# Two heads' score products in the two row halves of TensorE, with readers that take two PSUM banks at once

## The chip, the cores and the metric

The kernel runs on one core of one Trainium2 chip. The core has five engines with instruction queues of their own: TensorE (PE in the profile, with its weight loads as PEld), VectorE (DVE), ScalarE (ACT), GpSimd (POOL) and SyncE (SP), which here issues nearly all DMAs. The metric is device time in microseconds (us) from one execution of the whole program; several executions are timed and their median is taken.

## What is computed

A transformer layer in fp32 on one sequence of 2048 tokens with 512 channels: layer norm, attention with 32 heads of 16 channels in a sliding window of 256 tokens, an output projection with a residual, a second layer norm, and a mixture of 8 experts of hidden size 1376, two for each token.

```python
def _A_ref(x, wqkv, wo):            # H = 32, Dh = 16, W = 256
    qkv = (x @ wqkv).reshape(B, S, 3, H, Dh).transpose(2, 0, 3, 1, 4)
    q, k, v = qkv[0], qkv[1], qkv[2]
    scores = jnp.einsum("bhqd,bhkd->bhqk", q, k) * (Dh ** -0.5)
    mask = (idx[:, None] - idx[None, :] >= 0) & (idx[:, None] - idx[None, :] < W)
    p = _softmax(jnp.where(mask[None, None], scores, -1e9), axis=-1)
    o = jnp.einsum("bhqk,bhkd->bhqd", p, v)
    return o.transpose(0, 2, 1, 3).reshape(B, S, D) @ wo

h = x + _A_ref(_layernorm(x), A_wqkv, A_wo)
out = h + _B_ref(_layernorm(h), B_wg, B_w1, B_w2)
```

`_B_ref` takes the two experts with the largest gates for each token, applies gelu(x w1) w2 for each, and adds them up with normalised gates.

## The kernel before, in words

Matrices are held as a high and a low part in fp32r, so that a dense product is three products (high·high, high·low, low·high). The sequence is cut into four chunks of 512 tokens, and attention into 32 units: chunk c of 4 with head group g of 8, four heads to a group. A last stage runs the experts one after another.

A unit goes through these steps:

- `qk(u)` (line 535): twelve matmuls of 512 columns make Q and K of the group; ACT and POOL split them into high and low, three DMAs write them to DRAM (lines 547 to 549), and four read them back in another layout into one of four slots (lines 555 and 560). In a slot, heads 0 and 2 lie on partitions 0 to 47 (16 channels, as three products), heads 1 and 3 on partitions 64 to 111. Q has a plane for each of the four heads, and is zero on the partitions of the other head of its pair; K has one plane for a pair of heads.
- `maxes(u)`: for each of four blocks of 128 queries and each head, a matmul over 126 partitions makes 128 × 384 scores (fewer in chunk 0) in one PSUM bank (line 588). DVE copies the part above the diagonal from the far block with a predicate (line 594), so that 256 columns hold just the window, and takes their maximum (line 597). `fin` (lines 604 to 606) splits the negated maxima into two parts and transposes them; a DMA writes them to DRAM (line 609), and another reads them back into partitions 126 and 127 of Q (line 612), where K holds ones. So the second score product already has the maximum subtracted.
- `attend(u)`: scores again, transposed, over all 128 partitions (line 636), in four tiles A to D of key blocks (three tiles in chunk 0). Each of `scores()`'s groups fills one bank; ACT takes the exponential into the tile `PT` (line 640), POOL zeroes what lies outside the window (line 660), and PE multiplies with V (line 676). This last product uses 17 columns for each of four heads, placed in four column strips of the array, and adds up in the bank `oT`.
- `norm_and_v(c)` (V at line 482) and `project(c)` (lines 748 and 851, with the routing of the experts) run once for each chunk, among the units.

The order of work is not written out: every step is a task with an engine, an estimated duration, a priority and the buffers it needs, and `Plan.order()` runs a list schedule over them and emits the instructions of each engine in the order it finds. Engines then run their queues in order and wait on semaphores. Buffers are counted in pools: seven single PSUM banks (`one`), of which groups of maxima may hold three (`mx`) and groups of scores three (`ab`); the other tasks take from the same seven. `oT` is the eighth bank. On all engines a task is issued only when its buffers are free, and the PSUM bank of a group of scores or maxima is free again when ACT or DVE has read it for the last time.

## Time and profile before

| | us |
|---|---|
| median of 3 runs | 1243.21 |
| lowest and highest | 1240.88 and 1250.29 |
| the profiled execution's own time | 1246.75 |
| its span, first to last instruction | 1244.7 |

| engine | busy, share of the span | instructions |
|---|---|---|
| PE | 1118.5 us, 90% | 6801 |
| PEld | 892.2 us, 72% | 6801 |
| DVE | 678.2 us, 54% | 1833 |
| ACT | 540.8 us, 43% | 1153 |
| POOL | 455.1 us, 37% | 668 |

Attention runs from the first matmuls to some 640 us (the last P·V ends there), the experts from about 644 us to the end. PE's "busy" counts a matmul from its start to its modelled end; matmuls overlap in the array, so a busy PE is not an array at its peak. "Idle before" of a group is the time its engine stood still ahead of it, with what ended that time. The granted clock is the share of TensorE's full clock that the throttle allowed; over the span it was 0.948.

### The profile page before, as it was taken

The page shows a single profiled execution, that of the slowest core. Times are in us where ns is not written, and L with a number is a line of the kernel's source. Part 1 is how long each engine was busy: PE and PEld are TensorE (multiplying, and loading weights), DVE is VectorE, ACT ScalarE, POOL GpSimd, SP SyncE. Part 2 cuts the span into 40 slices and gives each one's busy share as a digit, 9 for nine tenths or more (in the row PEclk, how much of TensorE's full clock was granted, in tenths as well). Part 3 has the DMA queues.
Part 4 walks back from the last instruction along what each step waited for, and adds up shares of the span by engine and source line. Part 5 has one row for each costly group of instructions (what it writes and reads, how often), then busy time and mean ns, then how long its engine had stood idle before and what let it go on. Part 6 is the DMA issues. An engine that isn't in the chain of part 4 may idle for free.

```text
span 1244.7 us, 19621 instructions
## 1 busy us (share of the span) xinstructions
PE 1118.5 (90%) x6801; PEld 892.2 (72%) x6801; DVE 678.2 (54%) x1833; ACT 540.8 (43%) x1153; POOL 455.1 (37%) x668
## 2 busy tenths in 40 slices
PE   1797989979898999998788999999999999999994
PEld 0574666657666676766357889889798897989893
DVE  4288567977787786776546144434243342434341
ACT  1335555434554445544555245425253351626240
POOL 4734544744556464653844411220302112020101
PEclk9998998999899898996887899999999999999997
DMA  3489799884799758777332634442534334353422
GB/s 114 112 239 274 207 243 275 252 197 89 190 260 263 179 120 213 197 214 183 108 118 75 144 104 123 113 82 89 120 115 122 87 107 87 105 130 112 105 66 29
DMA packets 111617, 185.51 MB, mean 149 GB/s; under 512 B 25092, under 2 KB 44612, under 8 KB 111508
## 3 DMA queue, kind: packets, MB, share of 16 engines
q1 hardware_dynamic: 102852, 166.42, 47.7%
q0 software_dynamic: 8656, 17.73, 7.7%
q8 instruction: 56, 0.92, 0.3%
q14 instruction: 53, 0.43, 0.1%
HBM read 124.51 MB, written 59.60 MB: 148 GB/s over the span
## 4 chain that ended last, share of the span: by engine, by line
PE 67%; DMA 17%; DVE 6%; SPq 3%; POOL 2%; issue 2%; ACT 1%; POOLq 0%; DVEq 0%; ACTq 0%
PE one L1139 21%; PE one L1118 21%; PE one L588 5%; PE one L535 5%; PE oT L676 4%; PE one L636 4%; DMA mr<-qkd 3%; PE one L748 2%; PE one L482 2%; DMA md<-mt 2%; DMA mr<-md 2%; DMA od<-zone 1%; PE one L851 1%; SPq L387 1%; DVE mx L597 1%
## 5 line engine op out<-in xcount | busy, mean ns | idle before, releaser
L640 ACT ACTIVATE zone<-one 128x384 f32<-128x384 f32 (+1 forms) x480 | 207.8, 494 | 155.2 <-PE one L636 131.7
L1118 PE MATMUL one<-mr 128*128 128x256 f32 (+7 forms) x1980 | 269.2, 298 | 0.0
L1118 PEld LDWEIGHTS one<-mr 128*128 128x128 f32 (+1 forms) x1980 | 266.7, 188 | 1.1
L1139 PE MATMUL one<-zone,mr 128*128 128x512 f32 (+3 forms) x1080 | 260.4, 397 | 0.0
L660 POOL TENSOR_SCALAR_AFFINE_SELECT zone<-zone 128x256 f32<-128x256 f32 (+1 forms) x368 | 169.5, 483 | 201.4 <-ACT zone L640 198.8
L1139 PEld LDWEIGHTS one<-zone,mr 128*128 128x128 f32 (+3 forms) x1080 | 193.3, 181 | 53.0
L363 DVE TENSOR_TENSOR mr<-one,mr 128x256 fp32r<-128x256 f32 (+9 forms) x205 | 100.5, 494 | 180.1 <-ACT mr L361 171.2
L597 DVE TENSOR_REDUCE mx<-one 128x1 f32<-128x256 f32 (+2 forms) x472 | 192.3, 426 | 0.8
L588 PE MATMUL one<-mr 126*128 126x384 f32 (+2 forms) x512 | 166.1, 376 | 19.9 <-DMA mr<-qkd 10.7
L636 PE MATMUL one<-mr 128*128 128x384 f32 (+1 forms) x592 | 152.9, 336 | 21.1 <-DMA mr<-md 11.2
L594 DVE COPY_PREDICATED one<-above,one 128x128 f32<-128x128 uint32 x448 | 120.8, 289 | 77.3 <-PE one L588 68.7
L588 PEld LDWEIGHTS one<-mr 126*128 126x128 f32 x512 | 95.7, 201 | 78.1 <-issue 25.9
L636 PEld LDWEIGHTS one<-mr 128*128 128x128 f32 x592 | 109.6, 204 | 48.6 <-DVE mx L597 17.0
L361 ACT CAST mr<-one 128x256 fp32r<-128x256 f32 (+9 forms) x205 | 87.6, 431 | 128.8 <-PE one L1090 113.6
L1085 POOL DMA_INDIRECT mf<-xnd,tb x36 | 35.1, 975 | 287.6 <-PE one L1090 271.4
L535 PE MATMUL one<-mr 128*128 128x512 f32 x384 | 108.8, 413 | 23.2 <-ACT mr L361 23.0
L361 ACT CAST mr<-mf 128x512 fp32r<-128x512 f32 (+4 forms) x120 | 93.2, 787 | 82.2 <-DMA mf<-in_B_w_dram 26.1
L1123 ACT ACTIVATE one<-one 128x256 f32<-128x256 f32 (+7 forms) x165 | 65.2, 395 | 142.7 <-PE one L1118 132.6
L1145 DVE TENSOR_SCALAR mf<-one,tb 128x512 f32<-128x512 f32 (+3 forms) x36 | 27.0, 750 | 173.2 <-PE one L1139 173.2
L1147 POOL DMA_INDIRECT out_dram<-mf,tb x36 | 61.5, 1708 | 162.2 <-DVE mf L1145 142.6
L676 PE MATMUL oT<-zone 128*17 128x384 f32 (+2 forms) x1408 | 110.9, 407 | 8.1 <-POOL zone L660 6.9
L365 POOL TENSOR_TENSOR mr<-mf,mr 128x512 fp32r<-128x512 f32 (+2 forms) x74 | 94.1, 1284 | 55.4 <-ACT mr L361 50.6
(141 smaller groups left out, 965.6 us busy)
## 6 DMA issues: line engine op xcount, KB each, us to landing
mf<-in_B_w_dram SPq DMA_DIRECT2D x32, 688.0 KB
mf<-in_B_w_dram SPq DMA_DIRECT2D x40, 512.0 KB
qkd<-mr SPq DMA_DIRECT2D x32, 512.0 KB
mr<-qkd SPq DMA_DIRECT2D x80, 192.0 KB
mr<-qkd SPq DMA_DIRECT2D x48, 288.0 KB
mr<-wgd SPq DMA_DIRECT2D x24, 512.0 KB
mf<-in_A_x_dram SPq DMA_DIRECT2D x32, 256.0 KB
qkd<-mr SPq DMA_DIRECT2D x64, 128.0 KB
```

The costliest lines, as they stand in the source:

```text
L361: a = add("ACT", 51 + n * 0.86, lambda: nc.scalar.copy(dst_h(), src()), deps, prio, bufs)
L363: b = add("DVE", 65 + n * 1.05, lambda: nc.vector.tensor_sub(dst_l(), src(), f32(dst_h())), [a], prio, bufs)
L535: nc.tensor.matmul(single[bk.h], wt()[:, int(i == 1), k * 128:(k + 1) * 128], xt[:, k], start=(i == 0 and k == 0), stop=(i == 2 and k == 3))
L588: nc.tensor.matmul(view()[:, j], Q[slot.h][0:126, h + j, b * 128:(b + 1) * 128], K[slot.h][0:126, (h + j) // 2, (b + k0) * 128:(b + 3) * 1 ...
L594: nc.vector.copy_predicated(t[:, :, n - 128:n], above.unsqueeze(1).to_broadcast([128, m, 128]), src)
L597: nc.vector.tensor_reduce(mx_t[slot.h][:, h:h + m, b], view()[:, :, max(0, n - 256):n], axis=AX.X, op=OP.max)
L636: nc.tensor.matmul(single[bk.h][:, off:off + w], K[slot.h][:, h // 2, r * 128:(r + 1) * 128], Q[slot.h][:, h:h + hs, b * 128:(b + m) * 128 ...
L640: return add("ACT", 51 + n * 0.833, lambda: nc.scalar.activation(dst(), single[bk.h][:, 0:n].rearrange(order, q=128, **({"h": 2} if "h" in ...
L660: nc.gpsimd.affine_select(v, v, pattern=[[0, v.shape[1]], [-1 if far else 1, 128]], compare_op=OP.is_gt if far else OP.is_ge, fill=0.0, ba ...
L676: nc.tensor.matmul(oT[32 * j:32 * j + 17, b * 128:(b + n) * 128], V[blk % NV][:, 4 * g + j, :], PT[pt.h][j // 2][:, off:off + n, j % 2], s ...
L1118: nc.tensor.matmul(bank(), a[:, k, f * 128:f * 128 + w], b[:, k, :n], start=(i == 0), stop=(i == 11))
L1139: nc.tensor.matmul(single[bk.h][:n], h[a][:w], spot["w2"][b][f][:w], start=(f == 0 and q == 0), stop=(f == NF - 1 and q == 2))
```

## The change

Q and K of a slot now hold both heads of a pair in one plane: head 2i on partitions 0 to 47, head 2i + 1 on partitions 64 to 111, without zeros between. A score product uses just the 48 partitions of its head (50 in `attend`, with the two rows of the maximum, which now lie behind each half at partitions 48 and 112). The two matmuls of a pair stand one behind the other in PE's queue, in row halves 0 and 64 of the array, and write to two neighbouring banks. Six of the seven banks become three tiles of two banks; a `Buf` of size 2 takes an even and the next odd place of the pool, and a `Buf` of size 1 prefers a place whose neighbour is taken. DVE's predicated copy and its maximum and ACT's exponential each take both banks in one instruction. `mx` and `ab` go from three to two. `PT` has its head dimension ahead of its block dimension, and POOL's selection and the P·V product are addressed to match. The read of the maxima is two DMAs of two rows each, and the write puts them down transposed. The zeroing of Q is gone.

```diff
@@ class Plan
-        def places(p, e):
-            return [f for f in self.free[p] if f[1] + self.HOP[f[2]][e] <= now]
+        def places(bufs, e):
+            out, used = [], set()
+            for b in bufs:
+                can = [f for f in self.free[b.pool] if f[1] + self.HOP[f[2]][e] <= now and (b.pool, f[0]) not in used]
+                at = {f[0]: f for f in can}
+                if b.size == 2:
+                    f = next(((f, at[f[0] + 1]) for f in can if f[0] % 2 == 0 and f[0] + 1 in at), None)
+                else:
+                    alone = [f for f in can if f[0] ^ 1 not in at]
+                    f = (alone or can)[:1]
...
@@ layer
-        Q.append(take(mr, 4, 512))
+        Q.append(take(mr, 2, 512))
         K.append(take(mr, 2, 768))
+        at[id(mr)] += 1024
-    PT = [[take(zone, 3, 2, 128) for _ in range(2)] for _ in range(NPT)]
+    PT = [[take(zone, 2, 3, 128) for _ in range(2)] for _ in range(NPT)]
-    single = [psum.tile([128, 512], F32, name=f"one{i}", bufs=1) for i in range(7)]
+    dual = [psum.tile([128, 2, 512], F32, name=f"two{i}", bufs=1) for i in range(3)]
+    single = [dual[i // 2][:, i % 2] for i in range(6)] + [psum.tile([128, 512], F32, name="one", bufs=1)]
-    plan = Plan(dict(xn=4, wgs=2, hl=1, qk=NQ, pt=NPT, osb=1, one=7, mx=3, ab=3, oT=1,
+    plan = Plan(dict(xn=4, wgs=2, hl=1, qk=NQ, pt=NPT, osb=1, one=7, mx=2, ab=2, oT=1,
-        memsets[i] = [add(en, 1742, lambda i=i, eng=eng: eng.memset(f32(Q[i]), 0.0), [], pr),
-                      add(en, 1315, lambda i=i, eng=eng: eng.memset(f32(K[i]), 1.0), [], pr)]
+        memsets[i] = [add(en, 1315, lambda i=i, eng=eng: eng.memset(f32(K[i]), 1.0), [], pr)]
@@ qk
-                nc.sync.dma_start(f32(Q[slot.h])[par * 64:par * 64 + 48, par::2],
+                nc.sync.dma_start(f32(Q[slot.h])[par * 64:par * 64 + 48],
@@ maxes
-            m = 512 // n
-            for h in range(0, 4, m):
-                bk, lim = Buf("one"), Buf("mx")
+            m = 2 if n <= 256 else 1
+            for h in range(0, 2, m):
+                bk, lim = Buf("one", 2), Buf("mx")
...
-                    for j in range(m):
-                        nc.tensor.matmul(view()[:, j], Q[slot.h][0:126, h + j, b * 128:(b + 1) * 128],
-                                         K[slot.h][0:126, (h + j) // 2, (b + k0) * 128:(b + 3) * 128], start=True, stop=True)
+                    for j in range(h, h + m):
+                        for a in range(2):
+                            r = slice(64 * a, 64 * a + 48)
+                            nc.tensor.matmul(view()[:, a, j - h], Q[slot.h][r, j, b * 128:(b + 1) * 128],
+                                             K[slot.h][r, j, (b + k0) * 128:(b + 3) * 128], start=True, stop=True)
...
-                a = add("PE", m * max(107, mm_ns(n)), mm, qk_read[u], pp, [slot, bk, lim])
-                a = add("DVE", 69 + 133 * m, cp, [a] + made, pp, [bk, lim])
-                reds.append(add("DVE", 65 + m * min(n, 256) * 1.041, red, [a] + reds[-1:], pp, [bk, lim]))
+                a = add("PE", m * max(107, mm_ns(n) + 20), mm, qk_read[u], pp, [slot, bk, lim])
+                a = add("DVE", 135 + 266 * m, cp, [a] + made, pp, [bk, lim])
+                reds.append(add("DVE", 135 + 2 * m * min(n, 256) * 1.041, red, [a] + reds[-1:], pp, [bk, lim]))
...
-            box["d"] = dram.tile([128, 32], F32, name=f"md{u}")
-        w = dma(lambda: nc.sync.dma_start(box["d"], mt_t[slot.h]), 30000, [f], p + 1, [slot])
-        def rd_():
-            nc.sync.dma_start(f32(Q[slot.h])[126:128].rearrange("p h (b i q) -> p (h b) i q", b=4, i=4),
-                              ap(box["d"], 0, [[512, 2], [32, 16], [1024, 4], [1, 32]]))
-        m_read[u] = [dma(rd_, 20000, [w], p + 1.1, [slot], 625)]
+            box["d"] = dram.tile([32, 128], F32, name=f"md{u}")
+        w = dma(lambda: nc.sync.dma_start(ap(box["d"], 0, [[32, 4], [128, 32], [1, 32]]), mt_t[slot.h]), 30000, [f], p + 1, [slot])
+        m_read[u] = [dma(lambda par=par: nc.sync.dma_start(f32(Q[slot.h])[par * 64 + 48:par * 64 + 50].rearrange("p h t -> p (h t)"),
+                                                           ap(box["d"], par * 1024, [[2048, 2], [1, 1024]])), 20000, [w], p + 1.1, [slot])
+                     for par in range(2)]
@@ attend
+            for pr in range(2):
+                pp = p + pr / 8
+                bk, lim = Buf("one", 2), Buf("ab")
+                parts_ = sorted(parts, key=lambda t: t[2], reverse=name == "A")
+                def mm(parts_=parts_, bk=bk, pr=pr):
                     off = 0
+                    for r, b, m in parts_:
+                        for a in range(2):
+                            rows = slice(64 * a, 64 * a + 50)
+                            nc.tensor.matmul(dual[bk.h // 2][:, a, off:off + m * 128], K[slot.h][rows, pr, r * 128:(r + 1) * 128],
+                                             Q[slot.h][rows, pr, b * 128:(b + m) * 128], start=True, stop=True)
+                        off += m * 128
+                pe = add("PE", sum(max(107, mm_ns(m * 128) + 20) for _, _, m in parts_), mm, m_read[u] + qk_read[u], pp, [slot, bk, pt, lim])
+                exps = add("ACT", 115 + 768 * 0.833, lambda bk=bk, pt=pt, pr=pr: nc.scalar.activation(
+                    PT[pt.h][pr].rearrange("p h b q -> p h (b q)"), dual[bk.h // 2][:, :, 0:384], AF.Exp, scale=0.25), [pe], pp, [bk, pt, lim])
...
```

More of the change, by code (lines that the diff above doesn't have):

```diff
@@ L91, in order @@
                     x = heapq.heappop(ready[e])
-                    need = {}
-                    for b in x[2].bufs:
-                        if b.h is None:
-                            need[b.pool] = need.get(b.pool, 0) + 1
-                    if all(len(places(p, e)) >= k for p, k in need.items()):
+                    where = places([b for b in x[2].bufs if b.h is None], e)
+                    if where is not None:
                         got = x[2]
```

77 lines of the change are left out of this document (30 added, 47 removed).

## The prediction

> **What bounds the kernel now.** I read the page from its head, then busy time by stretch, then the groups of instructions with shapes kept apart, then a short timeline of PE, and last what PE waited for at the two score lines.
>
> ```profile
> span 1244.7 us, 19621 instructions
> PE 67%; DMA 17%; DVE 6%; SPq 3%; POOL 2%; issue 2%; ACT 1%; POOLq 0%; DVEq 0%; ACTq 0%
> ...
> 150.00:250.00 100.00, 91.33 (x589) 65.93 (x590) 78.40 (x244) 52.36 (x116) 52.67 (x89) 0.93 0.92 251
> 450.00:550.00 100.00, 92.73 (x625) 66.19 (x624) 68.99 (x229) 53.64 (x119) 60.31 (x104) 0.95 0.74 191
> 550.00:650.00 100.00, 82.88 (x529) 53.75 (x527) 58.49 (x170) 51.94 (x115) 53.86 (x93) 0.83 0.55 148
> ...
> 700.00:1244.00 544.00, 527.80 (x3105) 465.95 (x3105) 208.31 (x339) 214.75 (x447) 91.19 (x67) 0.98 0.39 102
> ```
>
> The columns of the last rows are PE, PEld, DVE, ACT and POOL busy, then the granted clock, DMA share and GB/s. From 700 us on the experts keep PE busy for 527.80 of 544 us; nothing there is edited. The change lives in the attention stage, some 50 to 650 us. There PE is the busiest engine (91.33 of 100 us), DVE follows (78.40), ACT is at half, the DMA engines are at 0.92 and 0.74 of their time. The chain gives PE 67% and DMA 17%. So PE sets the pace, but a busy PE is not a streaming PE. The timeline shows the true pace:
>
> ```profile
> 442.95 0.84 PE L676 MATMUL oT<-zone 128*17 128x384 f32 x8
> ...
> 448.58 0.52 PE L636 MATMUL one<-mr 128*128 128x256 f32 x3
> 448.94 0.52 PE L588 MATMUL one<-mr 126*128 126x384 f32 x2
> 449.29 1.09 PE L535 MATMUL one<-mr 128*128 128x512 f32 x4
> 450.22 0.39 PE L636 MATMUL one<-mr 128*128 128x256 f32 x2
> 450.54 1.09 PE L676 MATMUL oT<-zone 128*17 128x128 f32 x16
> 451.56 0.44 PE L588 MATMUL one<-mr 126*128 126x384 f32 x1
> 451.84 0.29 PE L636 MATMUL one<-mr 128*128 128x256 f32 x1
> ```
> ```profile
> L676 PE MATMUL oT<-zone 128*17 128x384 f32 x512 | 57.3, 518 | 0.0
> L676 PE MATMUL oT<-zone 128*17 128x256 f32 x448 | 39.6, 402 | 2.8 <-POOL zone L660 2.8
> ```
>
> Columns of the first: start, length, engine and line, tile, shape of the first, count; of the second: busy time, mean ns of one, idle before. One 384-column matmul lasts 0.34, but two take 0.52: the second starts 0.18 behind the first. Three of 256 columns take 0.52 and each lasts 0.28, so 0.12 apart; four of 512 in 1.09 are 0.23 apart. The P·V product (L676), four matmuls at a time in column strips, does eight of 384 columns in 0.84; one lasts 0.52, so groups of four are 0.32 apart, 0.11 for each 128 columns. It also shows what a change of the array's shape costs. The last L636 starts at 450.22 + 0.39 − 0.28 = 450.33, and L676 only at 450.54, 0.21 later in place of 0.12: 0.09 to go in. L676 ends at 451.63; its last group, of 256 columns, lasts 0.40, so it began at 451.23, and a follower was due 0.21 later, at 451.44. L588 starts at 451.56, some 0.10 late, lasts 0.44 in place of 0.34, and its successor starts 0.28 later in place of 0.18. Leaving costs 0.10 and another 0.10 for a weight load that could not be prefetched: 0.20.
>
> **The change, part by part.** These rows price it (out of the groups by shape; busy time, then mean ns of one, then idle before):
>
> ```profile
> L588 PE MATMUL one<-mr 126*128 126x384 f32 x448 | 155.8, 388 | 16.6 <-DMA mr<-qkd 8.2 <-DMA mf<-xd 4.1 <-DVE mx L597 3.5
> L588 PE MATMUL one<-mr 126*128 126x256 f32 x32 | 7.0, 318 | 0.0
> L588 PE MATMUL one<-mr 126*128 126x128 f32 x32 | 4.6, 267 | 3.2 <-DMA mr<-qkd 2.6 <-ACT zone L640 0.7
> L636 PE MATMUL one<-mr 128*128 128x384 f32 x256 | 81.7, 371 | 6.6 <-DMA mr<-md 3.6 <-ACT zone L640 1.5 <-DVE mx L597 1.1
> L636 PE MATMUL one<-mr 128*128 128x256 f32 x336 | 74.5, 310 | 14.5 <-DMA mr<-md 7.6 <-DVE mx L597 5.1 <-ACT zone L640 1.8
> L594 DVE COPY_PREDICATED one<-above,one 128x128 f32<-128x128 uint32 x448 | 120.8, 289 | 77.3 <-PE one L588 68.7 <-PE oT L676 3.4 <-issue 0.5
> L594 DVE COPY_PREDICATED_SCALAR one<-above,low 128x256 f32 x16 | 7.5, 476 | 2.6 <-PE one L588 2.6
> L597 DVE TENSOR_REDUCE mx<-one 128x1 f32<-128x256 f32 x448 | 176.1, 413 | 0.7
> L597 DVE TENSOR_REDUCE mx<-one 128x2 f32<-128x512 f32 x16 | 10.9, 682 | 0.0
> L640 ACT ACTIVATE zone<-one 128x384 f32<-128x384 f32 x256 | 111.8, 494 | 81.1 <-PE one L636 72.9 <-POOL zone L660 4.6 <-DVE lg L853 2.0
> L640 ACT ACTIVATE zone<-one 128x512 f32<-128x512 f32 x112 | 67.4, 601 | 47.2 <-PE one L636 33.8 <-issue 7.1 <-POOL zone L660 2.6
> L640 ACT ACTIVATE zone<-one 128x256 f32<-128x256 f32 x112 | 43.2, 386 | 26.9 <-PE one L636 25.0 <-issue 1.7
> L660 POOL TENSOR_SCALAR_AFFINE_SELECT zone<-zone 128x512 f32<-128x512 f32 x112 | 71.8, 647 | 98.3 <-ACT zone L640 96.2 <-DMA qkd<-mr 1.2
> ```
>
> *PE, score products.* Before: 448 + 256 matmuls of 384 columns at 0.18 and 32 + 32 + 336 narrower ones at 0.12: 126.7 + 48.0 = 174.7 us of streaming. After, with the two heads of a pair side by side: 224 + 128 pairs of 384, and 16 + 16 + 112 pairs of 256 or 128 columns for the maxima and the wide parts, 112 for the narrow parts that two heads no longer share: 352 × 0.18 + 256 × 0.12 = 94.1. Saved 80.6 us. No row shows two row halves at once; the nearest is L676, sixteen matmuls in column strips in 1.09 us, four at a time. Upper bound: no overlap, nothing saved. I take full overlap.
>
> Beside that stands a measurement of the Trainium skill (TensorE: Matmul & The Clock Gate, "Measured speedup vs the span model"): four row tiles gave 3.07 times, not 4. Were a pair as much less than ideal, it would cost 0.18 / 0.77 = 0.23, an estimate, and some 28 us of the saving would be gone. No run here shows it; the sum goes by the rows.
>
> *PE, changes of shape.* The built order of PE's instructions, from the first maximum to the last P·V, has 237 changes of shape before, all around L676, and 449 after: 199 into row halves, 130 into the full array, 120 into column strips. At 0.09 into strips and 0.20 into the others: 119 × 0.09 + 118 × 0.20 = 34.3 before, 120 × 0.09 + 329 × 0.20 = 76.6 after: +42.3. Lower bound 0, should a row split need no drain.
>
> The rows above are of column strips. The Trainium skill (TensorEngine Tiling (Array Packing), "Key Properties") says that a change of tiling mode drains the engine, and makes no difference between rows and columns; by it the 42.3 stands, without it the sum would be lower by that much. The trace agrees for strips (0.09 and 0.20).
>
> *PSUM, the part I weigh most.* Before, scores and maxima use seven single banks, up to three each. After, each group takes two neighbouring banks: three such pairs serve both, at most two each, and V, Q·K and projection groups sometimes sit in half of one. A pair is back with PE only after its reader: for scores 0.34 of the last matmul and one exponential of 768 elements, 494 + 384 × (601 − 386)/256 = 0.82: 1.16 us (before 0.34 + 0.49 = 0.83). For maxima 0.34, a copy over 256 elements (7.5 / 16 = 0.47 of busy time) and a maximum over 512 (10.9 / 16 = 0.68): 1.49 (before 0.34 + 0.27 + 0.39 = 1.00). A stretch of the new order (its number there, the line in the changed file, the pair of banks, the matmuls, what the first waits for):
>
> ```
> 1075 L654 two_75 128x256 x2, 1077 128x128 x2 [waits Activation]
> 1078 L601 two_74 128x384 x2 [waits DVE]
> 1080 L601 two_76 128x384 x2 [waits DVE]
> 1082 L654 two_75 128x384 x2 [waits Activation]
> ```
>
> Scores (L654) take pair 75, two groups of maxima (L601) follow, and the next scores want pair 75 again, 0.12 + 0.18 + 0.18 = 0.48 us after their predecessor's last matmul began, though it is back only after 1.16. PE is in order: behind that wait stand all its later groups, P·V and the projections too. I walked both orders with the spacings, the shape prices and these return times, charging each shortfall, and 0.10 for the weight load that a wait exposes: 7 us in 23 of 952 groups before, 89 us in 147 of 480 after. **+82 us.** It leaves out readers that are late with other work; if each returns 0.6 later, it is 35 and 170, so +135. Lower bound 0, if they only replace waits that stand there today.
>
> ```profile
>   DVE mx L597: 23.2, 24
>   ACT zone L640: 18.1, 41
>   DMA mr<-md: 15.6, 9
> ...
>   DVE mx L597: 21.6, 39
>   ACT zone L640: 19.9, 28
>   DMA mr<-qkd: 10.7, 5
>   DVE one L594: 6.6, 11
> ```
>
> Idle before L636 and L588, with what ended it: 23.2 + 18.1 + 21.6 + 19.9 + 6.6 = 89.4 us today end with DVE or ACT, far above the 7 of the walk. Those come from readers that are late, so the true answer may add to them or replace them. The 15.6 + 10.7 us for DMAs shrink if PE comes later; I count half as absorbed, −13.
>
> *DVE and ACT.* Per two maximum groups of 384: 2 × (289 + 413) − (476 + 682) = 246 ns less, × 224 = 55 us of DVE (of the shapes before and after, a copy with a tensor source taken like the one with a scalar); ACT 128 × (2 × 494 − 820) + 112 × (601 + 386 − 820) = 40 us. Neither is the bound, so they count only through the return times above.
>
> *The rest, at nothing.* Masks: POOL has as many elements, in four runs in place of one for the 512-element form; were they 2 × 412 − 647 = 0.18 dearer, 20 us over 112, hidden under POOL's own wait for ACT (98.3 us idle before that form alone). Zeroing Q's buffers leaves POOL's queue at the start; POOL is 2% of the chain, so nothing is counted for it.
>
> ```profile
> L660 POOL TENSOR_SCALAR_AFFINE_SELECT zone<-zone 128x256 f32<-128x256 f32 x256 | 98.1, 412 | 103.1 <-ACT zone L640 102.6
> L609 SPq DMA_DIRECT2D md<-mt x32: 319/338/2398, 68.0 to 610.8; - x32
> L612 SPq DMA_DIRECT2D mr<-md x32: 625/657/726, 69.9 to 614.6; - x32
> ```
>
> The read of the maxima becomes two DMAs: one more issue on SP of 0.34 to 0.66 us, 32 times, 11 to 21 us of a queue; queued behind it are the next unit's loads. The read itself goes from 128 pieces to four rows. SP is no part of the limit in the chain (SPq 3%), so ±5.
>
> **Sum.** −80.6 + 42.3 + 82 − 13 = **+31 us** on the profiled execution, which took 1246.75 us by its own time (span 1244.7, 2 us around it). The median of the three runs is 3.5 us lower, 1243.2: forecast 1274.
>
> **The rivals.**
> *The bank waits replace today's waits (faster).* For it: the 89 us are there already, and DVE and ACT have 55 and 40 us less to do. Against: return times grow by a third and more, and three pairs are fewer places than six banks. If all 82 fall on time already lost, −80.6 + 42.3 = −38: 1205; with three quarters, 1225. It decides from about half on, where the change is worth nothing. Chance 0.22 for beyond 1%, and 0.12 that it comes out even.
> *Weight loads of the two halves follow each other (slower).* An exposed load is 0.10, so two are 0.20, and no pair takes less: 352 × 0.02 + 256 × 0.08 + 199 entries × 0.10 = 47 more than forecast: 1321. For: loads in PE's timeline follow one another. Against: strips in L676 start together. Chance 0.10.
> *Readers late by 0.6 (slower).* +135 for +82: 1327. For: DVE at 78 of 100 us. Chance 0.09.
> *The halves do not overlap at all*: the change does not do what it says, 80.6 more than forecast: 1355. Chance 0.05.
> That leaves 0.42 for the forecast.
>
> **Numbers.** This kernel's runs lie from 1240.88 to 1250.29, so about 1% can be told from no change. Slower by over 1% (above 1256): 0.42 + 0.10 + 0.09 + 0.05 = 0.66. Within: 0.12. Faster: 0.22. The range runs from 1210, nearly the whole gain, to 1335, the two late cases; the forecast's own is 1256 to 1310.
>
> **What would show it.** Side by side: the two matmuls of a pair start within some ns, and pairs 0.18 apart. Shape: gaps of 0.20 before the first matmul of a row-half group behind a projection. Banks: idle of PE (and PEld) before the two score lines that ends with ACT and DVE grows from 89 to 150 us or more, while exponentials last 0.82 and the maximum 0.68. Wrong I am if this idle time stays below 110 and PE's busy share in 150 to 550 us falls with a shorter stage. A lower granted clock in the attention stage (0.83 in its last stretch now) would add to any wait and is not priced.

## The result

The changed kernel takes 1425.05 us (median of four runs, 1421.6 to 1430.28) against 1246.75 us for the kernel before beside it (four runs, 1240.88 to 1255.36): 1.1427 times as long, 95% interval 1.1344 to 1.1511. The forecast was 1274 us, with a range up to 1335: slower, as forecast, but by 178 us in place of 31.

From the page of the changed kernel, the head and the chain of waits by engine:

```profile
span 1421.0 us, 19104 instructions
...
PE 59%; DMA 12%; DVE 10%; ACT 8%; POOL 3%; issue 3%; SPq 3%; DVEq 0%; ACTq 0%; POOLq 0%
```

PE has 59% of the chain (67% before), DMA 12% (17%). What is new is DVE at 10% (6%) and ACT at 8% (1%): PE now waits for the engines that read PSUM. Busy time by stretch, with the columns of the prediction, first the changed kernel, then the kernel before:

```profile
60.00:650.00 590.00, 500.78 (x3194) 280.13 (x3194) 379.32 (x833) 251.16 (x358) 286.67 (x480) 0.81 0.73 194
150.00:250.00 100.00, 81.72 (x566) 45.52 (x566) 67.00 (x144) 46.95 (x69) 51.03 (x83) 0.93 0.86 246
450.00:550.00 100.00, 84.41 (x537) 46.77 (x535) 52.52 (x118) 40.58 (x58) 44.32 (x83) 0.76 0.61 149
550.00:650.00 100.00, 75.75 (x487) 40.85 (x483) 62.84 (x149) 37.77 (x50) 52.82 (x86) 0.74 0.57 157
706.00:1421.00 715.00, 589.99 (x3345) 500.75 (x3344) 241.62 (x458) 231.95 (x492) 117.91 (x102) 0.97 0.33 87
```
```profile
60.00:650.00 590.00, 525.55 (x3358) 371.91 (x3356) 423.24 (x1330) 292.21 (x642) 309.41 (x523) 0.92 0.76 201
635.00:1244.00 609.00, 580.54 (x3398) 509.09 (x3397) 246.22 (x469) 242.85 (x506) 116.36 (x103) 0.97 0.39 103
```

Two things are to be seen. In the attention stage (60 to 650 us) PE is busy for 500.78 us in place of 525.55, and its granted clock is 0.81 in place of 0.92. After the last P·V product PE used to stand still for 609 − 580.54 = 28 us; now it stands still for 715 − 589.99 = 125 us. The last P·V group of the timeline ends at 705.3 us (634.9 before). So of the 176.3 us by which the span grew (1421.0 − 1244.7), 70.4 lie ahead of that point, and 105.9 behind it, in the experts, of which the prediction said that nothing there is edited.

Timeline of PE in the changed kernel, columns as before:

```profile
500.18 1.48 PE L681 MATMUL oT<-zone 128*17 128x256 f32 x16
...
502.39 1.20 PE L546 MATMUL one<-mr 128*128 128x512 f32 x4
503.51 0.44 PE L601 MATMUL two<-mr 48*128 48x384 f32 x2
503.79 0.34 PE L654 MATMUL two<-mr 50*128 50x384 f32 x2
504.06 1.02 PE L681 MATMUL oT<-zone 128*17 128x384 f32 x8
...
506.67 0.44 PE L601 MATMUL two<-mr 48*128 48x384 f32 x2 [0.95 <-ACT zone L658]
507.15 1.20 PE L546 MATMUL two<-mr 128*128 128x512 f32 x4
```

The halves do overlap: a pair (x2) of 384 columns lasts 0.44 or 0.34, no longer than one matmul did before, and its two matmuls start 3 ns apart (median over the 397 pairs that lie in full-clock stretches and start within 50 ns). The shapes cost what was forecast: the four projection matmuls (L546) end at 503.59, the last lasts some 0.40 (1.09 − 3 × 0.23, from the row of four in the prediction) and so began at 503.19; the maxima follow 0.32 later in place of 0.23, the scores behind them 0.28 later in place of 0.18, and P·V 0.27 later in place of 0.18: 0.09 and 0.10 to go into the halves, 0.09 into the strips. The last but one row shows a wait of 0.95 us for ACT ahead of a group of maxima.

Groups by shape in the changed kernel, and what PE (with its weight loads) waited for ahead of the two score lines, first the maxima (L601), then the scores (L654):

```profile
L658 ACT ACTIVATE zone<-two 128x768 f32<-128x768 f32 x240 | 192.7, 811 | 252.6 <-PE two L654 206.3 <-POOL zone L665 11.2 <-DVE mt L623 9.4
...
L614 DVE TENSOR_REDUCE mx<-two 128x2 f32<-128x512 f32 x224 | 151.8, 686 | 4.3
...
L611 DVE COPY_PREDICATED two<-above,two 128x256 f32<-128x256 uint32 x224 | 93.8, 425 | 140.4 <-PE two L601 121.3 <-PE two L654 5.6 <-ACT zone L690 5.3
```
```profile
  ACT zone L658: 59.9, 67
...
  DVE mx L614: 25.3, 30
...
  DVE two L611: 1.1, 2
```
```profile
  ACT zone L658: 86.7, 90
  DVE mx L614: 38.2, 37
...
  DVE two L611: 2.8, 7
```

The readers (exponential, copy, maximum) last 0.81, 0.43 and 0.69 us (0.82, 0.47 and 0.68 forecast). Idle time of PE and PEld that ends with ACT or DVE: 59.9 + 25.3 + 1.1 + 86.7 + 38.2 + 2.8 = 214.0 us, against 92.6 before: the 89.4 of the prediction and 3.2 for DVE's copy ahead of the scores, which it left out.

Then the experts. One stretch of the changed kernel, all engines; L1123 is the first expert product, L1128 the Gelu in place on its bank, L373 and L375 split the result into a high and a low part:

```profile
868.22 0.53 DVE L375 TENSOR_TENSOR mr<-two,mr 128x352 fp32r<-128x352 f32 x1 [4.08 <-ACT mr L373]
868.78 0.37 ACT L1128 ACTIVATE two<-two 128x256 f32<-128x256 f32 x1 [0.59 <-DVE mr L375]
...
868.99 3.51 PE L1123 MATMUL two<-mr 128*128 128x256 f32 x24
...
872.53 0.37 ACT L1128 ACTIVATE two<-two 128x256 f32<-128x256 f32 x1 [2.14 <-PE two L1123]
...
873.34 0.43 DVE L375 TENSOR_TENSOR mr<-two,mr 128x256 fp32r<-128x256 f32 x1 [2.38 <-ACT mr L373]
873.80 0.45 ACT L1128 ACTIVATE two<-two 128x352 f32<-128x352 f32 x1 [0.49 <-DVE mr L375]
874.28 0.45 ACT L373 CAST mr<-two 128x352 fp32r<-128x352 f32 x1
...
874.76 0.53 DVE L375 TENSOR_TENSOR mr<-two,mr 128x352 fp32r<-128x352 f32 x1 [1.00 <-ACT mr L373]
...
875.34 0.89 PE L1123 MATMUL two<-mr 128*96 128x352 f32 x4 [1.42 <-DVE mr L375]
```

The trace leaves out the buffer's number; in the built program the rows of `two` from 868.99 on are the two halves of one two-bank tile. PE's groups in it end at 868.99 + 3.51 = 872.50. ACT takes the first half's Gelu at 872.53, but the second half's only at 873.80, right after DVE's last read of the *first* half (873.34 + 0.43 = 873.77), though it is another bank. PE then waits 1.42 us for DVE's last read of the second half (874.76 + 0.53 = 875.29) before it writes the first again at 875.34. The two halves of one tile are handled as one.

### The profile page after: what moved, and what is told of

Its sections match the earlier page's. It is cut to its first block, busy times and chain, and to the rows that moved or that the text cites. A ratio compares the mean times of both kernels' runs of the same rounds, so it can differ in the third digit from the quotient of the medians.

```text
span 1421.0 us, 19104 instructions
## 1 busy us (share of the span) xinstructions
PE 1162.7 (82%) x6913; PEld 825.7 (58%) x6913; DVE 650.7 (46%) x1369; ACT 522.0 (37%) x911; POOL 451.4 (32%) x664
## 4 chain that ended last, share of the span: by engine, by line
PE 59%; DMA 12%; DVE 10%; ACT 8%; POOL 3%; issue 3%; SPq 3%; DVEq 0%; ACTq 0%; POOLq 0%
PE two L1123 14%; PE two L1144 13%; PE one L1144 7%; PE oT L681 5%; PE two L654 4%; DVE mr L375 4%; PE one L546 4%; PE two L601 3%; ACT mr L373 3%; DMA mr<-qkd 3%; ACT two L1128 3%; PE one L493 2%; ACT zone L658 2%; DMA qkd<-mr 1%; DVE mx L614 1%
## 5 line engine op out<-in xcount | busy, mean ns | idle before, releaser
L658 ACT ACTIVATE zone<-two 128x768 f32<-128x768 f32 x240 | 192.7, 811 | 252.6 <-PE two L654 206.3
L1123 PE MATMUL two<-mr 128*128 128x256 f32 (+9 forms) x1428 | 210.4, 302 | 57.7 <-DVE mr L375 47.5
L1123 PEld LDWEIGHTS two<-mr 128*128 128x128 f32 (+1 forms) x1428 | 195.5, 187 | 72.1 <-DVE mr L375 57.7
L1144 PE MATMUL two<-zone,mr 128*128 128x512 f32 (+3 forms) x720 | 180.7, 402 | 23.4 <-DVE mr L375 12.3
L375 DVE TENSOR_TENSOR mr<-two,mr 128x256 fp32r<-128x256 f32 (+7 forms) x146 | 71.7, 494 | 233.5 <-ACT mr L373 190.8
L614 DVE TENSOR_REDUCE mx<-two 128x2 f32<-128x512 f32 (+1 forms) x240 | 167.0, 703 | 4.7
L1144 PEld LDWEIGHTS two<-zone,mr 128*128 128x128 f32 (+3 forms) x720 | 128.0, 182 | 67.9 <-DVE mr L375 17.3
L611 DVE COPY_PREDICATED two<-above,two 128x256 f32<-128x256 uint32 x224 | 93.8, 425 | 140.4 <-PE two L601 121.3
L654 PE MATMUL two<-mr 50*128 50x128 f32 (+2 forms) x704 | 121.6, 398 | 43.9 <-ACT zone L658 31.0
L654 PEld LDWEIGHTS two<-mr 50*128 50x128 f32 x704 | 74.1, 228 | 116.3 <-ACT zone L658 55.7
L601 PE MATMUL two<-mr 48*128 48x384 f32 (+2 forms) x512 | 114.1, 453 | 30.8 <-ACT zone L658 18.3
L1128 ACT ACTIVATE two<-two 128x256 f32<-128x256 f32 (+8 forms) x119 | 47.1, 396 | 215.2 <-PE two L1123 156.7
L373 ACT CAST mr<-mf 128x512 fp32r<-128x512 f32 (+4 forms) x120 | 92.5, 783 | 81.6 <-DMA qkd<-mr 23.7
L601 PEld LDWEIGHTS two<-mr 48*128 48x128 f32 x512 | 57.0, 221 | 94.2 <-ACT zone L658 41.7
L373 ACT CAST mr<-two 128x256 fp32r<-128x256 f32 (+7 forms) x146 | 62.4, 430 | 114.9 <-PE two L1144 53.8
L546 PE MATMUL one<-mr 128*128 128x512 f32 x264 | 84.2, 451 | 21.0 <-ACT mr L373 19.0
L1144 PE MATMUL one<-zone,mr 128*128 128x512 f32 (+2 forms) x360 | 86.6, 397 | 0.0
```

Source lines behind the costliest of these rows:

```text
L373: a = add("ACT", 51 + n * 0.86, lambda: nc.scalar.copy(dst_h(), src()), deps, prio, bufs)
L375: b = add("DVE", 65 + n * 1.05, lambda: nc.vector.tensor_sub(dst_l(), src(), f32(dst_h())), [a], prio, bufs)
L546: nc.tensor.matmul(single[bk.h], wt()[:, int(i == 1), k * 128:(k + 1) * 128], xt[:, k], start=(i == 0 and k == 0), stop=(i == 2 and k == 3))
L601: nc.tensor.matmul(view()[:, a, j - h], Q[slot.h][r, j, b * 128:(b + 1) * 128], K[slot.h][r, j, (b + k0) * 128:(b + 3) * 128], start=True, ...
L614: nc.vector.tensor_reduce(mx_t[slot.h][:, :, h:h + m, b], view()[:, :, :, max(0, n - 256):n], axis=AX.X, op=OP.max)
L654: nc.tensor.matmul(dual[bk.h // 2][:, a, off:off + m * 128], K[slot.h][rows, pr, r * 128:(r + 1) * 128], Q[slot.h][rows, pr, b * 128:(b + ...
```

## The experiments

Times are medians beside the kernel before on the same chip; "after P·V" is the span less the end of the last P·V; the clock is the one granted from 60 to 650 us, out of the row of that stretch.

| run | what it is | us | ratio to before, 95% interval | last P·V | after P·V | clock |
|---|---|---|---|---|---|---|
| before | | 1246.75 | | 634.9 | 609.8 | 0.92 |
| after | the change | 1425.05 | 1.143 [1.134, 1.151] | 705.3 | 715.7 | 0.81 |
| e1_oldest | after, experts take the longest-free bank | 1340.10 | 1.076 [1.062, 1.090] | 710.4 | 633.0 | 0.82 |
| e2_alone | before, with the placing rule | 1253.84 | 1.007 [1.004, 1.011] | 641.9 | 612.2 | 0.91 |
| e3_halves | before, row halves, two single banks a pair | 1331.10 | 1.069 [1.051, 1.087] | 719.4 | 617.4 | 0.79 |
| e4_dual | e1 with the full array | 1342.45 | 1.078 [1.067, 1.089] | 704.6 | 638.3 | 0.91 |
| e5_layout | before, side edits | 1250.65 | 1.005 [1.001, 1.009] | 637.2 | 611.9 | 0.91 |
| e6_minimal | e5, row halves, a bank for each head | 1286.73 | 1.033 [1.029, 1.038] | 674.9 | 611.0 | 0.79 |
| e7_shared | before, banks in shared tiles | 1323.28 | 1.062 [1.058, 1.067] | 688.3 | 632.9 | 0.94 |
| e8_shared_alone | e7 with the placing rule | 1415.18 | 1.136 [1.127, 1.146] | 703.2 | 714.1 | 0.94 |
| e9_twice | e3, each pair issued twice | 1363.39 | 1.099 [1.090, 1.108] | 752.6 | 607.5 | 0.88 |
| e10_even_experts | after, experts share no tile | 1315.18 | 1.061 [1.052, 1.069] | 701.3 | 610.3 | 0.83 |
| e11_even_all | e10, nearly no other group shares one | 1294.08 | 1.044 [1.035, 1.052] | 679.9 | 610.5 | 0.84 |
| e12_even_full | e11 with the full array | 1311.89 | 1.058 [1.050, 1.066] | 700.5 | 610.0 | 0.91 |

### First: which part of the change costs what

The changed kernel, with the experts' groups on the bank that is free longest:

```diff
-                    f = (alone or can)[:1]
+                    f = (can if b.oldest else alone or can)[:1]
...
-            bk = Buf("one")
+            bk = Buf("one", 1, True)
```

> The changed kernel, but the experts' groups take the bank that has been free longest, in place of one whose neighbour is taken. My theory (the placement rule of the shared pool makes the experts reuse few banks, so that PE waits for their readers; the attention stage loses by pairs of banks that come back late): the last P.V stays near 705 us, the stretch from there to the end goes from 716 back to about 610 us, total near 1320 (1305 to 1340). Rival (the experts lose because two banks are now one tile, so that one half waits for the readers of the other): the stretch stays above 690, total above 1400.

Measured 1340.1, at the upper end of the theory's range: the placing rule (a single bank is taken first where its neighbour is taken) costs the experts 715.7 − 633.0 = 83 us. The stretch of 633.0 lies between theory and rival: 23 us of loss stay there, which the theory doesn't explain.

The kernel before, with only the rule:

```diff
-                        f = places(b.pool, e)[0]
+                        can = places(b.pool, e)
+                        at = {x[0] for x in can}
+                        alone = [x for x in can if x[0] ^ 1 not in at] if b.pool == "one" else []
+                        f = (alone or can)[0]
```

> The kernel before, with only the rule that a single bank is preferred whose neighbour is taken; no pairs, no row halves. My theory: the experts lose about 100 us here too, total 1330 to 1400, the attention stage some of it at most. Rival (shared tiles of two banks): no loss, 1240 to 1260.

Measured 1253.84, 612.2 us after P·V: a miss, and where the rival put it. The rule gives the experts' first product three banks to rotate over there too, and it costs next to nothing. It needs something else of the change to do harm.

The kernel before, with row halves and without two-bank readers:

```diff
-                bk, lim = Buf("one"), Buf("mx")
+                bks, lims = [Buf("one"), Buf("one")], [Buf("mx"), Buf("mx")]
...
-                        nc.tensor.matmul(view()[:, j], Q[slot.h][0:126, h + j, b * 128:(b + 1) * 128],
+                            r = slice(64 * a, 64 * a + 48)
+                            nc.tensor.matmul(view(a)[:, j - h], Q[slot.h][r, j, b * 128:(b + 1) * 128],
...
-    plan = Plan(dict(xn=4, wgs=2, hl=1, qk=NQ, pt=NPT, osb=1, one=7, mx=3, ab=3, oT=1,
+    plan = Plan(dict(xn=4, wgs=2, hl=1, qk=NQ, pt=NPT, osb=1, one=7, mx=4, ab=4, oT=1,
```

> The kernel before with the row halves alone: the two matmuls of a pair write two banks that need not be neighbours, each bank has its own copy, maximum and exponential and comes back by itself; up to four banks each for maxima and scores. My theory (row halves save 80 us of streaming and cost 42 us of shape changes): total 1195 to 1240. Rival (the row halves themselves cost the attention stage its time, by draining and by a lower granted clock): above 1290.

Measured 1331.1, far above the theory and where the rival put it. With no shared tile and short readers, the attention stage is 84.5 us longer, at a clock of 0.79.

The other half alone: `e1_oldest` with the full array and zero-padded Q as before, but bank pairs and readers of two banks:

```diff
-                            r = slice(64 * a, 64 * a + 48)
-                            nc.tensor.matmul(view()[:, a, j - h], Q[slot.h][r, j, b * 128:(b + 1) * 128],
+                            r = slice(0, 126)
+                            nc.tensor.matmul(view()[:, a, j - h], Q[slot.h][r, 2 * j + a, b * 128:(b + 1) * 128],
```

> The changed kernel with oldest-first for the experts as in e1, and with the full array: Q has its zeros again and each score product uses 126 or 128 partitions, but pairs of banks, the readers over two banks and the limits stay. My theory (late pairs of banks are the loss in the attention stage): as slow as e1 or slower by up to 40 us, 1310 to 1380. Rival (row halves are the loss): 1240 to 1265.

Measured 1342.45, as the theory said. Each half of the change alone loses 88 and 99 us, and both together (`e1_oldest`) 97. So I looked for what they have in common.

### Second: side edits, row halves without pairs, shared tiles

The side edits that both hold (layout of `PT`, order of the maxima, their write transposed and their read in two DMAs), alone:

```diff
-    PT = [[take(zone, 3, 2, 128) for _ in range(2)] for _ in range(NPT)]
+    PT = [[take(zone, 2, 3, 128) for _ in range(2)] for _ in range(NPT)]
...
-        w = dma(lambda: nc.sync.dma_start(box["d"], mt_t[slot.h]), 30000, [f], p + 1, [slot])
+        w = dma(lambda: nc.sync.dma_start(ap(box["d"], 0, [[32, 4], [128, 32], [1, 32]]), mt_t[slot.h]), 30000, [f], p + 1, [slot])
```

> The kernel before with only the side edits that the two half-changes before this had in common (P with its head dimension ahead of its block dimension, maxima in a pair-wise order, written transposed and read back in two DMAs); full array, single banks, the old plan. Theory, these are free: 1235 to 1255 us, the last P.V within 8 us of 638. Rival, they are the common cost of the two half-changes (which took 88 and 99 us more than the kernel before and both held them): about 1330 us.

Measured 1250.65, ratio 1.0046: free within 1%, and the base for the next run, which adds row halves without bank pairs; a head's scores go to one bank of its own (in the tiles A and D this regroups the exponentials, from 512 and 256 columns to 384 each):

```diff
-                        nc.tensor.matmul(view()[:, j], Q[slot.h][0:126, h + j, b * 128:(b + 1) * 128],
-                                         K[slot.h][0:126, (h + j) // 2, (b + k0) * 128:(b + 3) * 128], start=True, stop=True)
+                    r = slice(64 * a, 64 * a + 48)
+                    for i_, j in enumerate(js):
+                        nc.tensor.matmul(view()[:, i_], Q[slot.h][r, j, b * 128:(b + 1) * 128],
+                                         K[slot.h][r, j, (b + k0) * 128:(b + 3) * 128], start=True, stop=True)
```

> The run with the side edits, and in it the score products in row halves, but each head's group in one bank of its own as before: no group needs two banks, readers take one bank, the old limits of three. Theory, row halves cost more than they save by themselves (a change of shape at every entry, and a clock that falls when the array streams for a smaller part of the time): 1290 to 1340 us, granted clock in the attention stage 0.75 to 0.88 (0.92 to 0.95 before). Rival, the need for two banks at a time is what cost in the run with row halves and pairs of single banks: 1205 to 1255 us, clock above 0.92.

Measured 1286.73, just under the theory's 1290, at a clock of 0.79: row halves lose 36 us here, with no pair of banks in play. But in this run the two heads of a pair are groups of their own, and only 372 times does a matmul of a row half start within 50 ns of the one before it, for 608 pairs (595 times in the changed kernel, 500 in `e3_halves`): part of the saving is missing, so the 36 us are not the price of row halves alone. `e3_halves` lies 44 us higher; its plan differs in that a group asks for two banks at a time.

The kernel before, with only the tiles changed that the banks belong to:

```diff
-    single = [psum.tile([128, 512], F32, name=f"one{i}", bufs=1) for i in range(7)]
+    dual = [psum.tile([128, 2, 512], F32, name=f"two{i}", bufs=1) for i in range(3)]
+    single = [dual[i // 2][:, i % 2] for i in range(6)] + [psum.tile([128, 512], F32, name="one", bufs=1)]
```

> The kernel before with one edit: six of its seven banks are the halves of three tiles of two banks; the plan, the order of places and every instruction stay as they were. Theory, the waits between instructions are kept for a tile as a whole, so that a user of one half waits for the user of the other: 1260 to 1320 us, with 620 to 645 us from the last P.V to the end (612 before). Rival, a half is tracked by itself: 1243 within 8 us.

Measured 1323.28, slightly beyond the theory's end. Not one operation differs from the kernel before, and it loses 78 us: 53.4 ahead of the last P·V, 23.1 behind it. What ACT waited for ahead of the exponentials (us, times), in the kernel before and then in this run:

```profile
  PE one L636: 131.7, 112
...
  DVE one L594: 0.9, 1
```
```profile
  PE two L637: 93.1, 81
  DVE two L595: 24.4, 40
  PE one L637: 18.8, 18
  DVE mx L598: 16.9, 22
  PE two L589: 14.7, 13
  PE two L536: 10.1, 15
```

An exponential reads what L636 (now L637) wrote, and before it waited for little else. L594 (now L595) and L598 are DVE's copy and maximum, L589 and L536 PE's products for maxima and Q·K, all in other banks: an exponential has no use for them, and yet DVE's copy alone is behind 24.4 us in 40 waits, where it was behind 0.9 in one. In the built program 183 of the 480 exponentials wait for DVE, in place of 54 of 480. The waits come with the program: they are kept for a tile, not for a bank. The Trainium skill (PSUM — Partial Sum Buffer, "PSUM bank collisions raise a hardware error") asks only that users of one bank, and of the same 32 partitions in it, be kept apart; different banks may be read and written at once. Separate tiles in the kernel before do just that.

With the placing rule on top:

```diff
-                        f = places(b.pool, e)[0]
...
+                        alone = [x for x in can if x[0] ^ 1 not in at] if b.pool == "one" else []
+                        f = (alone or can)[0]
```

> The run with halves of shared tiles, and in it the rule that a single bank is taken first where its neighbour is taken. Theory, the rule costs only because it gives the two halves of one tile to work that follows one another: 680 to 730 us from the last P.V to the end (612 with the rule and separate tiles, 716 in the changed kernel), 1340 to 1400 us in all. Rival, the experts of the changed kernel lose by something else (a low clock left over from the attention stage, or pairs): 1255 us within 15, and 610 to 640 us from the last P.V to the end.

Measured 1415.18, above the theory's 1400, with 714.1 us after P·V, as it said: that is nearly the changed kernel's 1425 and 715.7 without any row half, bank pair or longer reader. Rule and tiles make a square: neither 609.8 us after P·V, rule alone 612.2, tiles alone 632.9, both 714.1. The rule prefers a bank whose neighbour is taken, so it hands the two halves of one tile to groups that follow one another: in the built program the first expert product goes over one half of a tile, the lone bank and the other half of that tile, again and again. PE's idle time ahead of the first expert product, 720 to 1220 us, in `e2_alone` and in `e8_shared_alone`:

```profile
L1121 PE MATMUL one<-mr 128*128 128x256 f32 (+6 forms) x1811 | 243.5, 296 | 1.7 <-DVE mr L366 1.7
```
```profile
L1122 PE MATMUL two<-mr 128*128 128x256 f32 (+7 forms) x1006 | 148.8, 303 | 40.8 <-DVE mr L367 33.0 <-ACT mr L365 6.6 <-issue 1.2
...
L1122 PE MATMUL one<-mr 128*128 128x256 f32 (+5 forms) x480 | 72.3, 301 | 0.0
```

The groups in the lone bank `one` wait for nothing; those in halves wait 40.8 us, nearly all for the readers of DVE and ACT.

### Third: the clock, and the change without shared tiles

`e3_halves`, with every pair of score matmuls issued twice over the same values:

```diff
-                    for j in range(h, h + m):
+                    for j in [j for j in range(h, h + m) for _ in range(2)]:
...
-                    for r, b, m in parts_:
+                    for r, b, m, rep in [(*t, rep) for t in parts_ for rep in range(2)]:
...
-                        off += m * 128
+                        off += m * 128 * rep
```

> The run with row halves and pairs of single banks, and in it every pair of score matmuls issued twice, the second time over the same values; the plan is left as it was. That adds 94 us of streaming in row halves at full speed. Theory, the granted clock follows how much the array does, and fell because halves leave it less to do: the clock in the attention stage rises from 0.71 to 0.85 to above 0.88, and the time from 1331 us to 1340 to 1385. Rival, row halves or the changes of shape hold the clock down by themselves: it stays at 0.70 to 0.85, and the time is 1420 to 1460 us.

Measured 1363.39: between the medians 32 us more, between the profiled spans 23 (1336.8 to 1360.1), for some 94 us more of streaming; the interval of `e3_halves` is wide (22 us to each side), but the rival's 1420 lies outside. The rows of 60 to 650 us, `e3_halves` and then this run:

```profile
60.00:650.00 590.00, 529.24 (x3123) 301.08 (x3121) 374.71 (x1270) 255.17 (x560) 276.32 (x465) 0.79 0.73 190
```
```profile
60.00:650.00 590.00, 557.00 (x4132) 357.52 (x4134) 366.44 (x1228) 249.70 (x546) 261.01 (x442) 0.88 0.69 184
```

The clock rises from 0.79 to 0.88, at the edge of what the theory said; in the single stretches of 100 us it lies between 0.74 and 1.00. So more work in row halves brings the clock up, which speaks for an array that had too little to do. How much of the 94 us the clock gave back isn't shown: some of the added streaming may have fallen into waits that stood there anyway. The Trainium skill (TensorE: Matmul & The Clock Gate, "What's actually happening") has the gate throttled by default and released by activity. The trace agrees with that, 0.79 to 0.88, against the idea that two busy halves draw the clock down. But what the gate counts isn't settled. PE's busy share does not tell it: `e6_minimal` has PE busy for 544 of these 590 us at 0.79, `e8_shared_alone` for 504 at 0.94. All runs with row halves lie at 0.79 to 0.88, all with the full array at 0.91 to 0.94. That a matmul in half of the rows counts for less would fit; no run here shows it by itself.

This run also shows the pure spacing of pairs:

```profile
480.19 0.52 PE L639 MATMUL one<-mr 50*128 50x384 f32 x4
480.64 1.19 PE L535 MATMUL one<-mr 128*128 128x512 f32 x4
```

Two pairs of 384 columns take 0.52, exactly what two single matmuls took before: 0.18 apart.

Then the changed kernel with its groups kept apart, first in the experts, then for every single bank but the accumulators of the last projection. A group may take only the even half of a shared tile or the lone bank:

```diff
-                    f = (alone or can)[:1]
+                    f = ([x for x in can if x[0] % 2 == 0] if b.even else alone or can)[:1]
...
-                pb = Buf("one")
+                pb = Buf("one", 1, True)
```

> The changed kernel, and in it the experts' groups take only the even half of a two-bank tile or the lone bank, the one free longest first: four places, and no two of them in one tile. Theory, the experts lose time only by two groups in one tile: 610 to 625 us from the last P.V to the end (716 in the changed kernel, 633 with the longest-free place and shared tiles), 1312 to 1335 us in all. Rival, they lose by having fewer banks: 640 us or more, 1350 us or more in all.

> The run before this one, with the same restriction for the single banks of every stage but the four accumulators of the last projection: pairs take a whole tile, and other work shares none. Theory, shared tiles cost the attention stage too (53 us in the run that only shared them): last P.V at 665 to 695 us (705 in the changed kernel), 1280 to 1315 us in all. Rival, places for V and Q.K groups become scarce and take that back: last P.V at 700 us or later, 1315 to 1350 us.

Measured 1315.18 with 610.3 us after P·V: with four places in place of seven, the experts are back at the 609.8 of the kernel before, so they had lost by the sharing alone. And 1294.08, with the last P·V at 679.9 in place of 705.3. Both as the theory said.

The same restriction with the full array and zero-padded Q:

```diff
-                            r = slice(64 * a, 64 * a + 48)
+                            r = slice(0, 126)
...
-                            rows = slice(64 * a, 64 * a + 50)
+                            rows = slice(0, 128)
```

> The same restriction on the run with the full array and zero-padded Q, pairs of banks and readers of two banks (1342 us with shared tiles). Theory, most of that run's loss was the sharing: 1260 to 1300 us, granted clock 0.92 or more in the attention stage. Rival, it is the late return of bank pairs by the longer readers: 1315 to 1350 us, last P.V at 690 us or later.

Measured 1311.89, last P·V at 700.5: near the rival's low end, beyond the theory's 1300. Sharing was 30 us of `e4_dual`'s loss, 28 of them after the last P·V (638.3 to 610.0). Some 70 stay; they are the price of pairs with long readers together with that of the fewer places that the restriction leaves to V, Q·K and projections, which no run takes apart. PE's idle time (with its weight loads) ahead of the maxima (first fence) and of the scores in this run:

```profile
  DVE mx L614: 42.6, 43
  ACT zone L658: 31.2, 41
...
  DVE two L611: 3.4, 4
```
```profile
  ACT zone L658: 58.7, 58
  DVE mx L614: 28.9, 42
...
  DVE two L611: 5.7, 11
```

42.6 + 31.2 + 3.4 + 58.7 + 28.9 + 5.7 = 170.5 us end with ACT or DVE, 78 more than the 92.6 before. No run beats the kernel before.

## Why the prediction was right in direction and wrong in size

To weigh the terms I walked PE's matmuls in the traces from 60 us to the last P·V and split each distance between two starts: streaming at the spacings of the prediction, 0.09 for a change of shape and 0.10 more for the weight load behind an entry, what half clock adds to these, and the rest as waits. These are estimates by that rule. The clock records of these traces hold full and half clock only: between 60 us and the last P·V half clock stands for 92 us in the kernel before, 253 in the changed one, 208 in `e11_even_all` and 137 in `e12_even_full`. How much of this goes to the column of half clock, and how much to waits, hangs on the rule: a second walk that doubles every streaming and shape price at half clock finds +45 us for the clock in the changed kernel, where the table has +33.

| us | streaming | shapes | half clock | waits | total |
|---|---|---|---|---|---|
| before | 416 | 33 | 9 | 116 | 574 |
| after | 355 | 70 | 42 | 178 | 645 |
| e11_even_all | 357 | 72 | 35 | 156 | 619 |
| e12_even_full | 431 | 33 | 21 | 155 | 640 |

**"Nothing there is edited. The change lives in the attention stage": this step failed.** It took the experts for untouched because no line of theirs is in the diff. But the diff changes the tiles that their banks are cut from, and the rule by which they get them, and 105.9 of the 176.3 us are theirs. The prediction even said that V, Q·K and projection groups sometimes sit in half of a pair, and asked only whether a pair was free, not who then waits for whom. Shared tiles with the rule account for 1425 − 1294 = 131 us, measured in `e11_even_all` by undoing them and in `e8_shared_alone` (170 us) by adding only them. That the two differ may come from the pairs, which take whole tiles in the changed kernel and so share less; it was not tested. Without the sharing the change would be at 1294 us, 52 above the 1241.61 of the kernel before beside it and inside the 1256 to 1310 that the forecast gave itself. That it lies inside is partly luck: as the terms below show, the saving was too small and the clock was left out, and the bank waits were too large.

**Streaming** (−80.6): held in kind. Halves run side by side, 0.18 apart; the walk finds 92 us in row halves for the 94.1 forecast. All scores go from 163 to 92 us in it (it leaves out what lies ahead of 60 us), but P·V goes from 84 to 94, so 61 us are left of the saving. P·V's 1408 matmuls are the same in both kernels; their rows are longer at the lower clock (518 ns before at 384 columns, 592 after), so those 10 us may belong to the clock. This was not settled. The rival with serial weight loads falls, and so does the one without overlap. The factor of the Trainium skill that was weighed in the prediction (TensorE: Matmul & The Clock Gate, "Measured speedup vs the span model"), by which a pair would take 0.23, does not show at two halves: 0.18.

**Shapes** (+42.3): the trace has 446 changes in place of 237, +37 us by the walk. Held.

**Bank pairs** (+82, −13 for DMA waits): the wait is there, its size lies between. `e12_even_full` shows +78 in the idle time that ends with the readers, but this counts PE and its weight loads; by the walk all waits grow by 39 us there and by 40 in `e11_even_all`, against the 69 of the sum. In the changed kernel it is 62, with the sharing in it. The rival that pairs only replace today's waits falls as it was put: 214.0 us of idle time, not under 110, and the same sum over the two score lines is 205.1 in `e11_even_all`, without the sharing. But by the walk some of the forecast waits did fall on time that was lost already. The DMA waits ahead of the two score lines fell by more than the 13 counted, from 26.3 to under 3 us. That readers are 0.6 late was not tested alone.

**The granted clock** ("not priced"): +33 us by the walk, about half of what the attention stage lost (+26 in `e11_even_all`). It was named as open and left at nothing, though the saving itself takes work off the array. By the walk that is also why the −38 of streaming and shapes never came: in the setting of pairs row halves gain 18 us (`e12_even_full` to `e11_even_all`). With single banks they lose 36 (`e5_layout` to `e6_minimal`, where many pairs do not start together); there half clock stands for 246 us ahead of the last P·V in place of 99. That the lower clock is the cause of these losses is argued from the traces, not shown by a run that changes the clock alone.

**Side edits** (±5): 1250.65 against 1245.44, held.

By the walk `e11_even_all` is −59 + 39 + 26 + 40 = +46 us ahead of the last P·V (45 measured), where the sum had +31. The range failed for want of one mechanism, the shared tiles, not through a term of the sum. A two-bank tile whose halves are tracked apart was not tried; the kernel has no such tile.

## What to carry to other kernels

When a diff merges two buffers into one tile, list every other user of them, edited or not, and ask who then waits for whom; a placing rule that is harmless with separate tiles (`e2_alone`) cost 92 us with shared ones (1323.28 to 1415.18), and a run of the old kernel on the new tiles (`e7_shared`) tells it in one edit. If pairs are needed, let single users take only one half of a tile. Price the granted clock with a change that moves work into a part of the array: here it was lower in every run with row halves, and in no run that only made TensorE wait more (`e7_shared`, `e8_shared_alone`).

## What the runs showed of the hardware

Two matmuls of 48 or 50 partitions in the two row halves start 3 ns apart and take no longer than one. The runs with them had a lower granted clock, 0.79 to 0.84 in place of 0.91 to 0.94, which by the walk, an estimate, took back a part of the saving. Issuing the same pairs a second time cost some 32 us in place of 94, with 0.88.
